# Single-bank accumulators for the last stage, and an order of all steps that comes from a table

## The chip, the cores and the metric

The kernel runs on one core of a Trainium2 chip. Its engines work side by side, each through its own instructions in order: TensorE (PE in the profile; its loading of weights is PEld), VectorE (DVE), ScalarE (ACT), GpSimd (POOL) and SyncE (SP). GpSimd and SyncE issue most of the transfers. The matrix results land in PSUM, of which the kernel's program uses eight banks of 512 float32 columns over 128 partitions. The metric is the device time of one execution in microseconds; a lower one is better.

## What is computed

```python
# q, k, v: [8, 12, 448, 64], scaled by 0.1;  w_ch1: [768, 3072], w_ch2: [3072, 768]
scores = scale * np.matmul(q, k.transpose(0, 1, 3, 2))
attn = np.maximum(scores, 0.0) ** 2 / S
x = np.matmul(attn, v)                      # then [8, 448, 768]
X = np.fft.fft(x, axis=1)
X = np.fft.fft(X, axis=2)
u = x + np.real(X)
un = (u - mean(u)) / np.sqrt(var(u) + 1e-06)
out = u + np.maximum(un @ w_ch1, 0.0) @ w_ch2
```

Eight sequences (batches) go through an attention with a squared relu, a Fourier mixing over the sequence and the channels of which only the real part is kept, a normalisation, and a feed-forward part of two large products with a residual.

## The kernel before, in words

**Stages.** Per batch, heads are taken in pairs. q and k are loaded in row order and turned for TensorE (L623 does it by matmuls with an identity, L593 by transposing transfers); L954 forms the scores of a block of 128 keys, L967 puts a relu on them (ScalarE), L984 or L981 squares them (VectorE or ScalarE), L827 multiplies by v. L822 and L689 to L796 form sums and differences of channels (the Fourier transform is done on halves and quarters), L1432 and L1029 are the products with the cosine matrices, L1252 to L1277 put the parts together into the rows u, L1284 to L1290 find their mean and variance, L1287 (L1065 in batch 0) is the square root on ScalarE, and L1303 (L1102, L1107) writes the normalised rows `un`. These are turned: L1130, L1135 and L1205 by TensorE, L1380 by a transposing transfer from DRAM; the result is `unT`. L400 is a small activation that brings ScalarE the table of the square root.

**Feed-forward part.** The rows of all batches are cut into groups of 256 to 384 columns. A group's first product is L1930, whose results L1915 (VectorE) or L1917 (ScalarE) take out of PSUM with a relu into hidden rows `hT`; L1958, L1985 and L2071 are the second products, in chains of 12 to 24 matmuls, which the adds of L1623 (VectorE) sum onto the residual rows `o`. The two last pairs of groups (four groups in all) are computed as two joints: `joint()` at L1733 forms seven products where eight would be plain, from sums and differences of rows and weights. Each product of L1762 is three matmuls of 256 columns. Between products that go on in the same PSUM bank ScalarE copies the bank's state to SBUF (L1777), and VectorE adds a copy and a bank to the hidden rows (L1782); L1806 is the last relu of a bank.

**PSUM.** `BS` (L237) hands out three tiles of two banks each, `psS`; `BF` two tiles of one bank, `psF`. In the last stage `spread()` (L1708) takes the three two-bank tiles for good and hands out their six halves one by one, with the two `BF` tiles as seventh and eighth bank. The halves are views of one tile, and the order between a writer and a reader is kept by tile: a write to one half waits for the readers of the other half too.

**What sets the order.** Everything is written as generators. Each step says which engine it takes, for how long, what it depends on and which buffers it needs: `need(engine, dur, deps, bufs, ok)`. `Streams.run()` (L102) holds a modelled clock for each engine and always picks the step that could begin first, ties by rank; `HEAD` moves the start of some kinds of steps in some phases, and TensorE takes a filler step where the next would come more than 0.5 us later. What is picked is issued at once, so this sets each engine's order of instructions. Generators also choose by this clock: which of two engines does an eviction, a square or an add (`sooner`, L973), which bank or buffer is taken (`take`, L49), whether a chain opens in the wide tiles.

## Time and profile before

| | |
|---|---|
| median of three runs | 568.57 us (567.13 to 569.33) |
| span of the profiled execution | 566.4 us |
| TensorE busy, share | 556.5 us, 98% |
| VectorE busy, share | 436.2 us, 77% |
| ScalarE busy, share | 318.2 us, 56% |
| GpSimd busy, share | 195.9 us, 35% |
| moved from and to DRAM over the span | 82.41 MB, 157 GB/s |

The profiled execution's own time is its span of 566.4 us, which is 2.2 us under the median. A matmul's duration in the trace reaches until its results are in PSUM, so that consecutive ones overlap. In a row of the trace stand start, length, engine, line, what is written and read, how many instructions, and in brackets how long the engine had been idle before and on what. An idle time on the engine that is not the bound costs nothing by itself.

### The profile page before, as it was taken

The numbers are of one execution on the slowest core, as the hardware profiler recorded it, in microseconds if no ns is written. First come the engines' busy times: TensorE is split into PE (matmuls) and PEld (weight loads), VectorE is DVE, ScalarE is ACT, GpSimd is POOL, SyncE is SP. The second block draws the span as 40 slices with busy tenths as digits, with TensorE's granted clock in tenths as the row PEclk, the third lists the DMA queues.
The fourth block names the chain that finished last, engine by engine and source line by source line (L and its number), as shares of the span: only waits on it lengthen the run. The fifth ranks groups of instructions, "written<-read, shape, count | busy, mean of one in ns | idle before, by whom it ended". The sixth has DMA issues, their size and how long they took to land.

```text
span 566.4 us, 11147 instructions
## 1 busy us (share of the span) xinstructions
PE 556.5 (98%) x4171; PEld 350.1 (62%) x4171; DVE 436.2 (77%) x1016; ACT 318.2 (56%) x536; POOL 195.9 (35%) x281
## 2 busy tenths in 40 slices
PE   7999999999999999999999999999999999999997
PEld 4376556544465455556756757767678688668864
DVE  7976564987789978887997896888899957644762
ACT  5978762676745686585786637638515154015400
POOL 8966225523346234462545545222015000000000
PEclk9999999999999999999999999999999999999999
DMA  9999999979959988899899979956425421231012
GB/s 110 180 209 230 215 215 165 217 144 134 181 96 210 215 117 179 164 187 184 174 163 196 198 121 198 164 123 154 115 65 174 124 75 29 71 127 56 1 57 83
DMA packets 152688, 82.41 MB, mean 146 GB/s; under 512 B 118076, under 2 KB 147900, under 8 KB 152636
## 3 DMA queue, kind: packets, MB, share of 16 engines
q0 software_dynamic: 57056, 33.63, 43.0%
q1 hardware_dynamic: 95580, 48.09, 38.1%
q8 instruction: 32, 0.52, 0.4%
q14 instruction: 20, 0.16, 0.1%
HBM read 62.91 MB, written 26.25 MB: 157 GB/s over the span
## 4 chain that ended last, share of the span: by engine, by line
PE 86%; DMA 5%; DVE 4%; ACT 2%; POOL 1%; issue 1%; DVEq 0%; POOLq 0%; ACTq 0%
PE psF L1930 25%; PE psF L2071 20%; PE psS L1762 8%; PE psS L954 7%; PE psS L2071 5%; DMA kn<-in_k_dram 5%; PE psF L827 5%; PE psF L1985 4%; PE psS L1432 2%; PE psF L1762 2%; PE psF L1958 2%; PE psF L822 1%; PE psF L623 1%; DVE sq L984 1%; PE psS L827 1%
## 5 line engine op out<-in xcount | busy, mean ns | idle before, releaser
L1930 PE MATMUL psF<-unT,w 128*128 128x256 bf16 (+2 forms) x1152 | 165.3, 299 | 0.0
L967 ACT ACTIVATE sq<-psS 128x896 bf16<-128x896 f32 x168 | 144.1, 919 | 31.7 <-PE psS L954 31.2
L1930 PEld LDWEIGHTS <-w 128*128 128x128 bf16 x1152 | 110.9, 98 | 49.6 <-issue 5.2
L984 DVE TENSOR_TENSOR sq<-sq 128x896 bf16<-128x896 bf16 x144 | 88.9, 634 | 13.3 <-ACT sq L967 12.5
L2071 PEld LDWEIGHTS <-hT 128*128 128x128 bf16 x648 | 62.5, 98 | 44.1 <-issue 4.8
L1917 ACT ACTIVATE hT<-psF 128x512 bf16<-128x512 f32 (+2 forms) x121 | 59.6, 508 | 41.1 <-PE psF L1930 40.3
L1623 DVE TENSOR_TENSOR o<-psF,o 128x384 f32<-128x384 f32 (+1 forms) x78 | 42.6, 547 | 24.3 <-PE psF L2071 20.8
L2071 PE MATMUL psF<-w,hT 128*128 128x384 bf16 x336 | 59.7, 326 | 0.6 <-DVE o L1623 0.6
L954 PE MATMUL psS<-qkT 64*128 64x448 bf16 (+1 forms) x336 | 51.5, 354 | 1.0 <-DVE qkT L630 0.8
L1777 ACT COPY copies<-psS 128x256 f32<-128x256 f32 x57 | 19.9, 374 | 53.0 <-PE psS L1762 48.1
L689 DVE TENSOR_SCALAR xT<-psF 128x224 bf16<-128x224 f32 x60 | 20.6, 384 | 26.1 <-PE psF L827 26.1
L1275 POOL TENSOR_TENSOR u<-tp,xn 112x385 f32<-112x385 f32 (+2 forms) x14 | 14.5, 1037 | 72.6 <-DVE tp L1255 48.6
L476 POOL DMA_DIRECT2D qn<-in_q_dram x21 | 15.7, 747 | 57.7 <-DVE qkr L583 50.3
L827 PE MATMUL psF<-sq,vn 128*64 128x448 bf16 x246 | 33.0, 362 | 0.0
L954 PEld LDWEIGHTS <-qkT 64*128 64x128 bf16 (+1 forms) x336 | 12.9, 94 | 32.3 <-issue 26.4
L1762 PEld LDWEIGHTS <-w 128*128 128x128 bf16 x288 | 28.2, 98 | 4.7 <-issue 1.1
L451 POOL DMA_DIRECT2D kn<-in_k_dram x42 | 25.9, 626 | 10.3 <-DMA w<-in_moe_w_ch_dram 6.0
L1284 DVE BATCH_NORM_STATS2 stats<-u 112x6 f32<-112x384 f32 (+2 forms) x56 | 28.7, 543 | 0.8 <-POOL u L1275 0.6
L451 POOL DMA_DIRECT2D vn<-in_v_dram x42 | 26.1, 638 | 6.2 <-DMA w<-in_moe_w_ch_dram 5.4
L476 POOL DMA_DIRECT2D vn<-in_v_dram x24 | 18.9, 789 | 25.5 <-PE psS L954 25.4
L1303 ACT ACTIVATE un<-u,small 112x768 bf16<-112x768 f32 (+2 forms) x22 | 22.0, 1023 | 9.5 <-DVE small L1290 8.4
L1782 DVE CUSTOM_DVE_ANT_0 hT<-psS,copies 128x256 bf16<-128x256 f32 x37 | 15.0, 421 | 14.1 <-PE psS L1762 6.2
(238 smaller groups left out, 946.9 us busy)
## 6 DMA issues: line engine op xcount, KB each, us to landing
out_dram<-o SPq DMA_DIRECT2D x55, 192.0 KB, 2.3
qn<-in_q_dram POOLq DMA_DIRECT2D x21, 224.0 KB, 5.1
vn<-in_v_dram POOLq DMA_DIRECT2D x24, 192.0 KB, 5.6
w<-in_moe_w_ch_dram POOLq DMA_DIRECT2D x12, 384.0 KB, 11.8
w<-in_moe_w_ch_dram POOLq DMA_DIRECT2D x4, 1152.0 KB, 23.4
kn<-in_k_dram POOLq DMA_DIRECT2D x21, 192.0 KB, 5.9
utop<-u SPq DMA_DIRECT2D x12, 336.0 KB, 2.9
o<-utop SPq DMA_DIRECT2D x16, 192.0 KB, 3.7
```

Source lines behind the costliest of these rows:

```text
L451: nc.gpsimd.dma_start(out=t[par * Dh:(par + 1) * Dh, par::2], in_=at)
L476: nc.gpsimd.dma_start(out=to, in_=src[b, hs, 0:rows].rearrange("h (p j) d -> p h (j d)", j=j))
L827: nc.tensor.matmul(av[h * Dh:(h + 1) * Dh, 0:S], lhsT=vn_home[:, at:at + Dh], rhs=sq[:, h, :], start=start, stop=stop, skip_group_check=True)
L954: nc.tensor.matmul(sc[:, h, 0:S].rearrange("k (c q) -> k c q", c=4), lhsT=flat[ps, k0:k0 + KB], rhs=qT[ps, pair], start=True, stop=True)
L967: nc.scalar.activation(r, sc[:, :, 0:S], AF.Relu)
L984: nc.vector.tensor_tensor(r, r, r, op=ALU.mult)
L1284: nc.vector.bn_stats(stats[:n, hf, :], u[:n, hf * (D // 2):(hf + 1) * (D // 2)])
L1623: nc.vector.tensor_tensor(o[:, cols], pc[:, cols], o[:, cols], op=ALU.add)
L1762: nc.tensor.matmul(ps[:, 0:N], lhsT=lhs, rhs=rhs[:, m], start=(start and m == 0), stop=(stop and m == 2), skip_group_check=True)
L1917: nc.scalar.activation(hs, ps, AF.Relu)
L1930: nc.tensor.matmul(ph[:, i * N:(i + 1) * N], lhsT=w1_sb[m][hf][:, (jj + i) * 128:(jj + i + 1) * 128], rhs=unT[:, m, 0:N], start=(m == 0), ...
L2071: nc.tensor.matmul(pc[:, cols], lhsT=lhs[i], rhs=rhs[i][:, cols], start=(start and i == 0), stop=(i == KP - 1), skip_group_check=True)
```

## The change

Two things are changed. First, in the last stage: the wide tiles are taken from a pool of their own, which `spread()` closes once they are free; a new pool gives six tiles of one bank each. The six banks are the same; what differs is that each is a tile by itself.

```diff
+    wide = tc.psum_pool(name="pw", bufs=1)
+    wide_psum = wide.__enter__()
...
-    BS = Banks(3, lambda i: psum.tile([128, 2, 512], FP32, name="psS", tag=f"S{i}", bufs=1))
+    BS = Banks(3, lambda i: wide_psum.tile([128, 2, 512], FP32, name="psS", tag=f"S{i}", bufs=1))
...
         yield need("PE", 0.0, rows_mixed, [BS] * 3)
-        tiles, plain = [BS.take() for _ in range(3)], []
-        B8 = Banks(6, lambda i: tiles[i // 2][:, i % 2] if i < 6 else plain[i - 6])
+        plain = []
+        wide.__exit__(None, None, None)
+        ones = ctx.enter_context(tc.psum_pool(name="p1", bufs=1))
+        B8 = Banks(6, lambda i: ones.tile([128, 512], FP32, name="psS", tag=f"one{i}", bufs=1) if i < 6 else plain[i - 6])
```

Second, `run()` doesn't choose any more. A string of codes names, step by step, the place in the list of the generator that goes next; a second table overrides choices of engine, bank or buffer by a running count of the questions asked. Both were found beforehand by a local search.

```diff
-HEAD = {('attentions', 'PE', 2): -0.6, ('attentions', 'PE', 3): -0.6, ('attentions', 'PE', 4): 0.07, ('mix_rows', 'PE', 2): -0.05}
-PHASES = (48.0, 140.0, 290.0, 440.0)
+CODES = '0123456789ABCDEFGHIJKLMNOPQRSTUVWXY'
+ORDER = "".join((
+    '00900000020099999999999999999999991999999199991999991N102999999190992011OON011111MMF11F4400M4MMF',
...
+CHOICES = {
+    77: 2, 91: 0, 93: True, 98: 1, 107: 0, 121: False, 166: False, 177: False, 190: True,
...
+def chosen(x):
+    asked[0] += 1
+    return CHOICES.get(asked[0] - 1, x)
...
     def run(self):
         end = {}
-        while self.streams:
+        for code in ORDER:
...
-            if best[1][2][0] == "PE" and spare is not None and best[0][1] - spare[0][1] > 0.5:
-                best = spare
-            s = best[1]
+            s = self.streams[CODES.index(code)]
...
-        return wait[other] + d + SPARE < wait[usual] + du
+        return chosen(wait[other] + d + SPARE < wait[usual] + du)
```

Counted over the program, each engine has as many instructions of each line as before (one filler matmul of L2154 is added at the start). What is moved is the order: on TensorE 1790 rows out of 8344 stand in other places, on VectorE 569 of 1018, on ScalarE 205 of 538, on GpSimd 24 and on SyncE 239. From about 100 us on TensorE's order is the old one but for local exchanges, apart from the last stage. Lines in the new file are 48 to 52 higher: L2123 is L2071, L1814 is L1762, L1002 is L954, L1829 is L1777.

Near 258 us of the trace a product of the second feed-forward product follows on TensorE on one that ends in the bank that an add (L1623) has to empty. Before (`w_3`, `w_0`: quarters of a weight matrix; `hT`: hidden rows; the bracket is the engine whose semaphore it waits for):

```order
L2071 MATMUL psF<-w_3_1061,hT 128x384
L2071 LDWEIGHTS hT
L2071 MATMUL psF<-w_3_1061,hT 128x384
L2071 LDWEIGHTS hT
L2071 MATMUL psF<-w_3_1061,hT 128x384
L2071 LDWEIGHTS hT
L2071 MATMUL psF<-w_0_976,hT 128x384 [waits DVE_49]
```

The same place on TensorE in the new order, from behind the first of the score matmuls that follow the last `w_3` matmul:

```order
L1002 LDWEIGHTS qkT
L1002 MATMUL psS<-qkT 128x448
L1002 LDWEIGHTS qkT
L1002 MATMUL psS<-qkT 128x448 [waits Activation_49]
L1002 LDWEIGHTS qkT
L1002 MATMUL psS<-qkT 128x448
L1002 LDWEIGHTS qkT
L1002 MATMUL psS<-qkT 128x448 [waits Activation_49]
L1002 LDWEIGHTS qkT
L1002 MATMUL psS<-qkT 128x448
L2123 LDWEIGHTS hT
L2123 MATMUL psF<-w_0_1008,hT 128x384 [waits DVE_49]
```

Six score matmuls have moved in between the product and the one that waits for its add.

In the second batch's normalisation, near 98 to 103 us, ScalarE had this order before (`qs`: part of the mixed rows; `small`: mean and deviation of a block of rows):

```order
L1252 ACTIVATE qs<-psS 128x385
L1252 ACTIVATE qs<-psS 112x385
L1287 ACTIVATE small<-small,few 128x1 x2
L1303 ACTIVATE un<-u,small 128x768 x2
L1287 ACTIVATE small<-small,few 112x1
L1210 CAST unT<-psS 128x6x127
```

And ScalarE has this now:

```order
L1302 ACTIVATE qs<-psS 128x385
L1337 ACTIVATE small<-small,few 128x1
L1302 ACTIVATE qs<-psS 112x385
L1353 ACTIVATE un<-u,small 128x768
L1337 ACTIVATE small<-small,few 128x1
L1353 ACTIVATE un<-u,small 128x768
L1337 ACTIVATE small<-small,few 112x1
```

Each block's root now stands directly ahead of that block, but for one eviction, where two roots stood ahead of two blocks.

In the last stage, near 514 us, TensorE before (`chan`, `sumx`: buffers that hold normalised rows or their differences here; `w_n`: weights):

```order
L1762 MATMUL psF<-chan_116,w_0_0_477 128x256
L1762 LDWEIGHTS w_1_0_487
L1762 MATMUL psF<-chan_116,w_1_0_487 128x256
L1762 LDWEIGHTS w_2_0_495
L1762 MATMUL psF<-chan_116,w_2_0_495 128x256
L1762 LDWEIGHTS w_3_0_505
L1762 MATMUL psS<-sumx,w_3_0_505 128x256 [waits DVE_49]
```

The same product (the one with `sumx`) on TensorE now:

```order
L1814 MATMUL psS<-chan_119,w_0_0_439 128x256 [waits DVE_49]
L1814 LDWEIGHTS w_1_0_456
L1814 MATMUL psS<-chan_119,w_1_0_456 128x256
L1814 LDWEIGHTS w_2_0_493
L1814 MATMUL psS<-chan_119,w_2_0_493 128x256
L1814 LDWEIGHTS w_3_0_506
L1814 MATMUL psS<-sumx,w_3_0_506 128x256 [waits DVE_49]
```

It stands behind another product, and its wait is for the reader of its own bank, no longer for the reader of a second half.

73 lines of the change are left out of this document (46 added, 27 removed), and 18 rows, old and new, of the table CHOICES.

## Prediction, made before the changed kernel ran

> **What bounds the kernel now.** I read the page's busy shares first, then what TensorE waited for, then the stretches of the span around the longest of those waits.
>
> ```profile
> span 566.4 us, 11147 instructions
> ...
> PE 556.5 (98%) x4171; PEld 350.1 (62%) x4171; DVE 436.2 (77%) x1016; ACT 318.2 (56%) x536; POOL 195.9 (35%) x281
> ...
> PE 86%; DMA 5%; DVE 4%; ACT 2%; POOL 1%; issue 1%; DVEq 0%; POOLq 0%; ACTq 0%
> ```
>
> TensorE is busy 98% of the span, and the chain that ended last lies 86% on it. The last step is the sum's anchor: 566.4 us of span against a median of 568.57, so 2.2 us lie around the span or are this execution's luck, and I carry them along unchanged. TensorE is idle 566.4 - 556.5 = 9.9 us. A change that neither removes nor adds a matmul that matters can win from waits, not from work.
>
> ```profile
> 0.00:10.40 10.40, 7.62 (x69) 4.72 (x69) 7.58 (x21) 4.66 (x7) 9.12 (x19) 1.00 0.86 92
> ...
> 29.80:47.62 17.82, 17.26 (x202) 13.08 (x201) 12.83 (x37) 13.55 (x29) 10.90 (x15) 1.00 1.09 224
> 47.62:430.00 382.38, 380.31 (x2728) 225.94 (x2726) 311.45 (x709) 240.68 (x368) 150.54 (x191) 1.00 0.98 166
> 430.00:566.40 136.40, 132.01 (x1010) 98.15 (x1008) 86.00 (x213) 40.02 (x108) 6.76 (x6) 1.00 0.25 77
> ```
>
> In this table of stretches (window, its length, then the busy time of TensorE and of the other engines; the granted clock, third from the end, is full throughout) 2.8 us of the idle time lie before 10.4 us, 0.6 us between 29.8 and the first product of the feed-forward part at 47.62, 2.1 us in the next 382 us, and 4.4 us in the last stage and the tail. The list of waits names them:
>
> ```profile
> PE psS L1205 <- ACT un L1303: 1.0, 1, 1.0
> PE psF L2071 <- DVE o L1623: 0.9, 2, 0.6
> ...
> PE psS L1762 <- DVE hT L1782: 0.5, 2, 0.3
> ```
>
> A matmul is shown longer than it keeps the next from starting: of L2071 below, five stand in 0.98 us, each 0.326 long, so they start 0.163 apart. I therefore price a wait by the distance of two starts less the usual distance, which makes it 0.16 (L2071) or 0.15 to 0.17 (L1762) longer than the idle time printed.
>
> **The change, part by part.** The engines keep the same instructions, apart from one more filler matmul (L2154) at the start, where the tensor engine has nothing to do before the first data; it costs nothing. Engine choices come out with equal counts on each engine. So all terms are waits that go or come.
>
> *1. Single-bank tiles in the last stage (L1708 to L1715).* Before, two products share one tile, and the write of one waits for the reader of the other's half. Four places in the last stage show it:
>
> ```profile
> 475.61 0.49 PE L1762 MATMUL psS<-unT,w 128*128 128x256 bf16 x3
> ...
> 476.09 0.27 PE L1762 MATMUL psS<-unT,quarter 128*128 128x256 bf16 x1
> ...
> 514.04 0.49 PE L1762 MATMUL psF<-chan,w 128*128 128x256 bf16 x3
> ...
> 514.36 0.41 DVE L1782 CUSTOM_DVE_ANT_0 hT<-psS,copies 128x256 bf16<-128x256 f32 x1
> ...
> 514.83 0.60 PE L1762 MATMUL psS<-sumx,w 128*128 128x256 bf16 x4 [0.30 <-DVE hT L1782]
> ...
> 522.47 0.37 ACT L1777 COPY copies<-psS 128x256 f32<-128x256 f32 x1 [0.51 <-DVE hB L1782]
> 522.47 0.38 PE L1762 MATMUL psS<-chan,xT 128*128 128x256 bf16 x2
> ...
> 522.89 0.49 PE L1762 MATMUL psS<-sumx,w 128*128 128x256 bf16 x3
> ...
> 535.45 0.38 PE L1762 MATMUL psS<-chan,xT 128*128 128x256 bf16 x2
> ...
> 536.02 0.49 PE L1762 MATMUL psS<-chan,w 128*128 128x256 bf16 x3 [0.19 <-DVE hT L1782]
> ```
>
> Three matmuls that start 0.11 apart (0.49 = 2 x 0.11 + 0.27) would let the next start 0.33 after the first: expected 475.94, 514.37, 522.69 and 535.67, seen 476.09, 514.83, 522.89 and 536.02. The waits are 0.15 + 0.46 + 0.20 + 0.35 = 1.16 us, and in all four the reader waited for reads the other half. They go: -1.15.
>
> The new order of that stage is tighter, though. A product that continues in the same bank needs the copy of L1777 (or the relu of L1806) first. Before, 3 products of L1762 stand only two products (0.65 us) behind the end of the one whose copy they need; in the new order I count 16. The nearest case in the trace:
>
> ```profile
> 477.07 0.49 PE L1762 MATMUL psS<-sumx,w 128*128 128x256 bf16 x3
> ...
> 477.60 0.38 ACT L1806 ACTIVATE hB<-psS 128x256 bf16<-128x256 f32 x1
> ...
> 478.05 0.49 PE L1762 MATMUL psS<-chan,w 128*128 128x256 bf16 x3
> ```
>
> The product issued from 477.07 leaves the queue at 477.40, ScalarE reads it 477.60 to 477.98, and the next use starts at 478.05, 0.65 us later and without an extra wait. So such a spot costs nothing if ScalarE is free and what ScalarE still has to do if not. At 4 of the 16 the row ahead on ScalarE belongs to a product that ended only one product, 0.33 us, earlier; a copy of 0.37 then ends 0.04 late, and a start 0.05 late adds to it. From below the price is 0 (this row), from above a whole copy each, 16 x 0.37 = 5.9 us (the row at 522.47). It is nearest to the first, ScalarE being busy 40 of 136 us in this stretch: 4 x 0.09 + 12 x 0.01, about +0.5.
>
> *2. Order at 258 us.* A product of group chain L2071 takes the bank that VectorE's add L1623 must empty first, straight behind the product that the add reads:
>
> ```profile
> 257.22 0.98 PE L2071 MATMUL psF<-w,hT 128*128 128x384 bf16 x5
> ...
> 258.24 0.56 DVE L1623 TENSOR_TENSOR o<-psF,o 128x384 f32<-128x384 f32 x1
> ...
> 258.85 0.65 PE L2071 MATMUL psF<-w,hT 128*128 128x384 bf16 x3 [0.65 <-DVE o L1623]
> ```
>
> Start to start this costs 0.81 us. In the new order six score matmuls (L954) stand between: at 0.19 us a matmul (two of them in 0.38 us, from 49.24 to 49.62 below), some of them side by side, about 0.8 us in all. The next is late only if the add waits for a VectorE row ahead of it: -0.75, between -0.81 and 0.
>
> *3. Second normalisation of batch 1 at 102 us.* The turn L1205 waits for the row block L1303 on ScalarE:
>
> ```profile
> 93.75 0.43 DVE L583 COPY qkr<-kn 128x1024 bf16<-128x1024 bf16 x1 [1.48 <-DMA kn<-in_k_dram]
> 94.09 0.55 DVE L1255 TENSOR_TENSOR tp<-psS,qs 128x385 f32<-128x385 f32 x1
> ...
> 98.97 0.29 ACT L1287 ACTIVATE small<-small,few 128x1 f32<-128x1 f32 x1 [6.11 <-DVE small L1285]
> 101.11 0.29 ACT L1287 ACTIVATE small<-small,few 128x1 f32<-128x1 f32 x1 [1.85 <-DVE small L1285]
> 101.96 1.94 ACT L1303 ACTIVATE un<-u,small 128x768 bf16<-128x768 f32 x2 [0.55 <-DVE small L1290]
> ...
> 103.04 0.51 PE L1205 MATMUL psS<-ident,un 128*128 128x128 bf16 x6 [0.97 <-ACT un L1303]
> ```
>
> VectorE stands 1.48 us before the copy that waits for a load, and everything for the block is queued behind it; ScalarE takes both roots before the first block. In the new order L1255 and L1257 stand ahead of that copy, the same two for the other rows behind the first root, and the first block straight behind that root. From root to block took 101.96 - 101.40 = 0.56 us, so the block could start at 98.97 + 0.29 + 0.56 = 99.8, less 1.48 and two VectorE rows of 0.55: 97.2, and ends 0.97 later, at 98.2. The turn stands 18 matmuls of 0.163, 2.9 us, earlier: TensorE would come to it at 103.04 - 1.13 - 2.9 = 99.0, with 0.8 us to spare. The second block hangs on GpSimd's rows, ahead of which two load issues fewer stand, and comes out just about when TensorE needs it. Best case -1.13; worst, if loads land no earlier and the turn moves up 2.9 us, about +0.8 (2.9 less the 2.1 that the roots alone give). I take -0.6.
>
> *4. The head.* The root table (L400) moves behind the first copy of L1081:
>
> ```profile
> 35.37 1.28 ACT L400 ACT_TABLE_LOAD   x1
> ...
> 37.37 0.32 PE L1029 MATMUL psS<-pc,seqm 128*128 128x384 bf16 x1 [0.24 <-ACT u L1081]
> ```
>
> That wait (0.40 start to start) goes, and the last products of the channel stage stand a little earlier; but what TensorE turns next is set by GpSimd's three blocks, in order behind load issues:
>
> ```profile
> 42.27 0.98 POOL L1102 TENSOR_SCALAR un<-u,small 112x768 bf16<-112x768 f32 x1
> ```
>
> It ends at 43.25. Between 0 and -0.9 of the head can go (the 0.40 here, and 0.5, the largest other thing in this stretch, its 0.56 us of idle time); I take -0.4, this wait alone. Against it stand 16 transposes (L623) moved from behind the first half product (L1930) to ahead of it:
>
> ```profile
> 48.69 0.39 PE L623 MATMUL psF<-ident,qn 112*64 112x112 bf16 x8
> ...
> 48.80 0.56 DVE L1915 TENSOR_SCALAR hT<-psF 128x384 bf16<-128x384 f32 x1
> ...
> 49.24 0.55 PE L954 MATMUL psS<-qkT 128*128 128x448 bf16 x2
> 49.62 0.81 PE L1930 MATMUL psF<-unT,w 128*128 128x384 bf16 x4
> ```
>
> As work this is neutral. As cover it isn't: they hide L1915, which empties the bank that the next L1930 takes. Now only the two L954 (49.24 to 49.62, 0.38 us) do; TensorE would stand there at 48.69 + 0.38 = 49.07, VectorE is through at 49.36 and some 0.06 of signalling: +0.35, between 0 and +0.6.
>
> *5. The moved loads and transposes.* GpSimd's issues keep their order in the head; SyncE's are moved in 56 places, each of which keeps more distance than its transfer needs, but one: a transpose L1380 (unT) has about 5 us of matmuls between issue and first use where it had 11.
>
> ```profile
> DMA to landing us min/median/max: 2.3/3.4/6.9
> ```
>
> At the median it is in time, at the longest it costs 6.9 - 5.0 = 1.9. I take 0. All other swaps stand at 0; nothing in the trace prices them, so I bound them by the waits not named so far, 2.1 - 1.6 = 0.5 gained, and by one more wait like L1205's, 1.0 lost.
>
> Sum: -1.15 + 0.5 - 0.75 - 0.6 - 0.4 + 0.35 = -2.05. 568.57 - 2.05 = 566.5.
>
> **The rivals.** *Slower: the tight copies queue.* If ScalarE starts each of the 16 copies behind another one, each costs up to 0.37: 568.57 - 2.55 (the sum without its 0.5) + 5.9 = 571.9. For it speaks that relus and copies share ScalarE and arrive in twos; against it the spare time of that engine. It eats the whole gain from 0.16 us a spot, and makes the kernel slower by over 0.5% from (2.55 + 2.84) / 16 = 0.34.
>
> *No change: waits only move.* The loads set when batch 1's blocks and the head's blocks are ready (the 1.48 us before L583). If parts 3 and 4 give nothing, the L1915 wait comes and a transpose is late by its 1.9 us, the sum is -1.15 + 0.5 - 0.75 + 0.35 + 1.9 = +0.85, 569.4; without the late transpose 567.5.
>
> *Faster: each term at its good end.* -1.16 - 0.81 - 1.13 - 0.9 - 0.5 = -4.5, with no new wait: 564.1. For it: ScalarE's spare time, and the 9.9 us idle. Against: it needs all five.
>
> *TensorE isn't the bound at all.* The page "Perfetto Trace Analysis" of the Trainium skill (section "Identifying the Most-Contended Engine") says that matmul busy time is no measure of nearness to the limit and that the share of weight loading is better; by that, 62% (the row above), an order could win up to 566.4 - 350.1 = 216 us. The rows speak against it here: the five matmuls of 257.22 start 0.163 apart, evenly, so the columns stream without a gap. A time under 560 by this gets 0.01.
>
> **How the numbers follow.** Chances: forecast 0.46 (its own range 565.2 to 568.0), waits that move 0.18, faster 0.23, slower 0.12, the last one 0.01. The measurement can't tell less than about 0.5%, 2.84 us, from no change: the runs shown already spread over 567.13 to 569.33. Faster by more (under 565.73) is the faster rival and 0.05 of the forecast's own range, with the last one 0.29; slower by more is the slower rival and 0.02 of late transposes, 0.14; the rest 0.57. The range of 8 in 10 goes from 563.6, just under the faster rival, to 570.4, halfway to the slower one.
>
> **What the profile after would show.** Right: no wait of L1762 on a sum or copy of another product; no idle time before L2071 near 257 us; L1205 with under 0.3 us; a wait of some 0.2 us printed for L1930 on L1915 near 49 us. The chain of waits in the last stage would name ScalarE's copies L1777 with 0.1 us or less at a time. Wrong: L1762 idle for L1777 with more than 0.1 us at many places, or new waits on loads between 100 and 300 us, or a first product of the feed-forward part well after 47.6.

## The result: 0.7% slower, and the profile after

The changed kernel takes 572.15 us (median of four runs, 571.42 to 573.25) against 568.03 us for the kernel before in the same series: a ratio of 1.0072 with a 95% interval of 1.0051 to 1.0093, 4.1 us slower. The forecast was 566.5. The profiled execution took 572.8 us with a span of 571.0.

```profile
span 571.0 us, 11108 instructions
...
PE 555.1 (97%) x4167; PEld 351.5 (62%) x4172; DVE 431.8 (76%) x1016; ACT 317.8 (56%) x536; POOL 200.7 (35%) x281
...
PE 75%; DVE 6%; POOL 6%; issue 4%; DMA 4%; SPq 2%; ACT 1%; DVEq 0%; POOLq 0%; ACTq 0%
```

These are the span, the busy shares and the chain that ended last. TensorE has the same work; the chain lies 75% on it instead of 86%, and VectorE, GpSimd, transfers and issue have the rest. To see where, I cut both spans at the same three matmuls. The table of stretches of the kernel after (window, length, then busy time and number of instructions, TensorE first; granted clock third from the end):

```profile
0.00:49.45 49.45, 43.70 (x455) 27.24 (x455) 37.91 (x96) 38.31 (x61) 41.11 (x84) 1.00 1.11 171
49.45:285.26 235.81, 233.23 (x1578) 127.93 (x1581) 185.07 (x433) 153.56 (x237) 98.48 (x131) 1.00 1.09 172
285.26:451.68 166.42, 162.79 (x1254) 110.09 (x1253) 140.41 (x310) 93.66 (x144) 61.07 (x66) 1.00 0.81 152
451.68:571.00 119.32, 115.42 (x888) 86.22 (x885) 68.38 (x179) 32.23 (x96) 0.00 (x0) 1.00 0.22 67
```

The stretch of the kernel before that answers to the third line:

```profile
284.00:446.00 162.00, 161.79 (x1254) 109.91 (x1252) 140.00 (x310) 92.94 (x143) 58.91 (x65) 1.00 0.79 151
```

The four lengths were 47.62, 236.38, 162.00 and 120.40 before. So the head (all that comes before the first L1930) is 1.83 us longer, the next stretch 0.57 shorter, the third 4.42 longer and the last 1.08 shorter, 4.60 in sum, which is the difference of the spans. Part of the first two is work that changed sides: the 16 transposes L623 that the prediction named now stand in the head. In the third, TensorE had 0.21 us of idle time before and has 3.63 now. The list of waits names what ended them:

```profile
PE psF L1982 <- DMA unT<-nbot: 1.2, 1, 1.2
PE psF L2123 <- ACT hT L1969: 1.2, 1, 1.2
PE psF L1982 <- DVE hT L1967: 1.0, 2, 0.8
PE psS L1457 <- DVE fold L796: 1.0, 1, 1.0
PE psS L875 <- DVE sq L1034: 0.9, 1, 0.9
...
PE psS L1079 <- DVE small L1123: 0.7, 1, 0.7
```

L1982 is L1930 of the kernel before, L2123 is L2071, L1969 is L1917 and L1967 is L1915, L1457 is L1407, L796 is L748, L875 is L827, L1034 is L984, L1079 is L1029 and L1123 is L1073. None of these waits stood in the list of before, and none is a product of the last stage. The table prices the larger waits by the distance of two starts less the usual one, as in the prediction:

| place in the kernel after | what TensorE waits for | us |
|---|---|---|
| 32, 35 and 39 us, head | VectorE's folds, ScalarE's copies, the mean of a row block | 1.17, 0.82, 0.87 (the last was 0.40) |
| 51 and 55 us | relu L1915, relu L1917 on ScalarE | 0.43 and 0.94 |
| 200 us | a transposed group (`unT`) | 1.30 |
| 290 and 295 us | VectorE's copy L689, add L1623 | 0.44 and 0.37 |
| 341 us | VectorE's square L984 | 1.06 |
| 394 us | relu L1915 on VectorE | 0.93 |
| 444 and 447 us | relu L1917 on ScalarE, add L1623 | 1.37 and 0.40 |

The rows from 290 us on add up to 4.57 us, where the profile of before had one wait of some 0.3 us (at 296 us). That is nearly the whole of the 4.42 us of the third stretch.

Two rows in the head show how a wait arises that no list names as one. GpSimd has a row of two columns there (L411; in the kernel before it is L363):

```profile
25.80 3.48 POOL L411 TENSOR_SCALAR drow<-drow 128x2 f32<-128x2 f32 x1
...
25.12 1.68 DVE L1034 TENSOR_TENSOR sq<-sq 128x896 bf16<-128x896 bf16 x3
...
28.91 0.27 DVE L796 TENSOR_TENSOR fold<-xT 128x225 bf16<-128x225 bf16 x1
31.19 0.41 DVE L421 TENSOR_SCALAR dfty<-dfty 128x480 int32<-128x480 f32 x1 [2.00 <-POOL dfty L414]
```

Before, it took 0.61 us:

```profile
23.95 3.48 DVE L984 TENSOR_TENSOR sq<-sq 128x896 bf16<-128x896 bf16 x6
...
24.57 0.61 POOL L363 TENSOR_SCALAR drow<-drow 128x2 f32<-128x2 f32 x1
```

It now starts beside a run of VectorE rows that stand without a gap from 25.12 to 28.91 + 0.27 = 29.18, and ends at 29.28. VectorE, which needs what GpSimd makes of it, then stands 2.00 us, and the folds behind that row are late for TensorE. The page "SBUF — State Buffer" of the Trainium skill (section "Who interferes with whom") says that a VectorE instruction with two inputs in SBUF and a GpSimd instruction that reads SBUF exclude each other, the second being blocked until the first is through. The row after agrees, and shows more: it is held not for one VectorE row but until a run of twelve pauses. Such a run doesn't always do that, though: before, the same row took 0.61 us in the middle of six squares without a gap. What decides between the two isn't shown.

The other row is the table load that the prediction had going out of TensorE's way:

```profile
37.52 1.28 ACT L1115 ACT_TABLE_LOAD   x1
...
39.53 0.49 PE L1079 MATMUL psS<-pc,seqm 128*112 128x384 bf16 x2 [0.71 <-DVE small L1123]
...
45.33 0.29 ACT L448 ACTIVATE drow<-few 128x1 f32<-128x1 f32 x1
```

The activation that was to bring the table (L400, here L448) only comes at 45.33 us, behind the roots, so that the first root (L1065, here L1115) loads it. The load stands between the first copy and that root, instead of ahead of the copy, and TensorE waits for what comes after the root.

### The profile page after: what moved, and what is told of

It reads as the page before. It is cut to its first block, busy times and chain, and to the rows that moved or that the text cites. A ratio compares the mean times of both kernels' runs of the same rounds, so it can differ in the third digit from the quotient of the medians.

```text
span 571.0 us, 11108 instructions
## 1 busy us (share of the span) xinstructions
PE 555.1 (97%) x4167; PEld 351.5 (62%) x4172; DVE 431.8 (76%) x1016; ACT 317.8 (56%) x536; POOL 200.7 (35%) x281
## 4 chain that ended last, share of the span: by engine, by line
PE 75%; DVE 6%; POOL 6%; issue 4%; DMA 4%; SPq 2%; ACT 1%; DVEq 0%; POOLq 0%; ACTq 0%
PE psF L1982 22%; PE psF L2123 15%; PE psS L1814 8%; PE psS L1002 5%; PE psS L2123 5%; PE psF L2037 4%; PE psF L2010 4%; PE psF L875 4%; PE psF L1814 2%; PE psS L1482 2%; SPq L641 1%; DMA unT<-ntop 1%; PE psF L870 1%; DMA unT<-nbot 1%; POOL qk L524 1%
## 5 line engine op out<-in xcount | busy, mean ns | idle before, releaser
L1982 PE MATMUL psF<-unT,w 128*128 128x256 bf16 (+2 forms) x1147 | 164.8, 299 | 2.5 <-DMA unT<-nbot 1.2
L1982 PEld LDWEIGHTS <-w 128*128 128x128 bf16 x1152 | 110.9, 98 | 52.1 <-issue 8.1
L1034 DVE TENSOR_TENSOR sq<-sq 128x896 bf16<-128x896 bf16 x144 | 87.2, 626 | 12.9 <-ACT sq L1017 12.8
L2123 PEld LDWEIGHTS <-hT 128*128 128x128 bf16 x648 | 62.3, 98 | 45.5 <-issue 4.0
L1969 ACT ACTIVATE hT<-psF 128x512 bf16<-128x512 f32 (+2 forms) x121 | 59.6, 509 | 39.2 <-PE psF L1982 38.2
L2123 PE MATMUL psF<-w,hT 128*128 128x384 bf16 x336 | 60.2, 326 | 1.5 <-ACT hT L1969 1.2
L1002 PE MATMUL psS<-qkT 64*128 64x448 bf16 (+1 forms) x336 | 51.4, 354 | 1.3 <-ACT sq L1017 0.8
L1829 ACT COPY copies<-psS 128x256 f32<-128x256 f32 x57 | 20.0, 375 | 48.5 <-PE psS L1814 47.9
L524 POOL DMA_DIRECT2D kn<-in_k_dram x21 | 16.0, 764 | 49.3 <-DVE qkr L631 41.1
L1002 PEld LDWEIGHTS <-qkT 64*128 64x128 bf16 (+1 forms) x336 | 13.0, 94 | 32.7 <-issue 28.2
L875 PE MATMUL psF<-sq,vn 128*64 128x448 bf16 x246 | 32.7, 362 | 0.0
L1814 PEld LDWEIGHTS <-w 128*128 128x128 bf16 x288 | 28.2, 98 | 3.8
L499 POOL DMA_DIRECT2D kn<-in_k_dram x42 | 25.8, 621 | 9.2 <-PE psS L1002 5.3
L499 POOL DMA_DIRECT2D vn<-in_v_dram x42 | 26.5, 640 | 5.0 <-DMA w<-in_moe_w_ch_dram 3.8
L875 PEld LDWEIGHTS <-vn 128*64 128x64 bf16 x288 | 13.0, 108 | 21.5 <-issue 17.5
```

Of the source, the lines that this page charges most:

```text
L499: nc.gpsimd.dma_start(out=t[par * Dh:(par + 1) * Dh, par::2], in_=at)
L524: nc.gpsimd.dma_start(out=to, in_=src[b, hs, 0:rows].rearrange("h (p j) d -> p h (j d)", j=j))
L875: nc.tensor.matmul(av[h * Dh:(h + 1) * Dh, 0:S], lhsT=vn_home[:, at:at + Dh], rhs=sq[:, h, :], start=start, stop=stop, skip_group_check=True)
L1002: nc.tensor.matmul(sc[:, h, 0:S].rearrange("k (c q) -> k c q", c=4), lhsT=flat[ps, k0:k0 + KB], rhs=qT[ps, pair], start=True, stop=True)
L1034: nc.vector.tensor_tensor(r, r, r, op=ALU.mult)
L1814: nc.tensor.matmul(ps[:, 0:N], lhsT=lhs, rhs=rhs[:, m], start=(start and m == 0), stop=(stop and m == 2), skip_group_check=True)
```

## The experiments

All runs write the order as a list of step names, so that stretches of the old and of the new order can be joined and single steps moved. In these kernels lines are 747 to 753 higher than in the kernel before. In most of them L2824 is L2071, L2683 is L1930, L2670 is L1917, L2668 is L1915, L2531 is L1782, L2374 is L1623, L2054 and L2051 are L1303 and L1300, L2038 is L1287, L2035 is L1284, L2026 and L2028 are L1275 and L1277, L2006 and L2008 are L1255 and L1257, L2003 is L1252, L1991 is L1240, L1735 is L984, L1718 is L967, L2183 is L1432, L1529 is L780, L2800 and L2802 are L2047 and L2049, L2040 and L2041 are L1289 and L1290, L2131 and L1342 are the transposes L1380 and L593, L2092 is L1341, a transfer that GpSimd issues, and L1200 is L451, the issue of a load. Times are compared by their ratios to the kernel before, which was run beside each.

### The two parts apart, and the last stage

The old order with single-bank tiles:

```diff
-ORDER = <steps of the new table>
+ORDER = <steps in the order of the kernel before>
```

> The old order on every engine, step for step, and only the six single-bank tiles of the last stage. If the waits on the other half are what the first term said, this gives -1.15 us against the kernel before (567.4 to 566.9, ratio about 0.998), and the four waits near 476, 515, 523 and 536 us are gone. If the new tiles cost something by themselves (the rival: the change itself, not the order, is what slows the kernel), it is 568 or more.

Measured 567.02 us, ratio 0.9985 (0.9959 to 1.001). In its trace the last stage is 1.17 us shorter than before, and L1762 waits for no sum of another product.

The new order with the old tiles of two banks:

```diff
-        ones = ctx.enter_context(tc.psum_pool(name="p1", bufs=1))
-        B8 = Banks(6, lambda i: ones.tile([128, 512], FP32, ...) if i < 6 else plain[i - 6])
+        tiles, plain = [BS.take() for _ in range(3)], []
+        B8 = Banks(6, lambda i: tiles[i // 2][:, i % 2] if i < 6 else plain[i - 6])
```

> The new order on every engine with the old two-bank tiles. If the order carries the whole loss and the tiles a small gain, this is the changed kernel's 572.15 plus the waits on other halves, which this order, being tighter, has more of: 573.3 to 575. If the tiles are the loss, it is near 568.

590.46 us, ratio 1.039 (1.0364 to 1.0417): 18 us more than the kernel after, and far above what was expected. What the halves cost depends on the order: 1.15 us in the old one, 18 in the tighter one. The list of waits has what the single banks remove (L2511 and L2531 are L1762 and L1782):

```profile
PE psS L2511 <- DVE hT L2531: 5.8, 7, 2.2
```

The old order up to the last stage, the new order in it:

```diff
-ORDER = <steps of the new table>
+ORDER = <old order, 2387 steps> + <new order of what is left>
```

> The old order up to the last stage, then the new order of the last stage with single-bank tiles. If a copy 0.65 us ahead of its reader costs nothing on a free ScalarE, this equals the kernel with the old order and single-bank tiles within 0.5 us (566.9 to 567.4). If the 16 tight places queue (the rival that forecast slower), they cost 0.1 to 0.37 us each: 568.5 to 572.

566.96 us, ratio 0.9981 (0.9971 to 0.9991), its last stage 1.12 us shorter than before. So by the traces the tiles give what was forecast, 1.15 us (in the times, the interval of the old order with single banks still holds no change); the new order of that stage gives nothing on top with single banks, and its tighter copies cost nothing.

### The head

The old order for the first 60 us, then the new one:

```diff
-ORDER = <steps of the new table>
+ORDER = <old order, 418 steps> + <new order of what is left>
```

> The old order up to about 60 us (batch 0 and the first products of the feed-forward part), the new order for all that is left. If the head's waits are a loss by themselves, the 2.6 us that the changed kernel is behind at 60 to 80 us go and stay gone: about 569.5. If later stages had slack that hides a late head, or the loss simply comes back (the rival), it stays at 571.5 to 572.5.

571.82 us, ratio 1.0062 (1.0043 to 1.008). The first L1930 still comes 1.07 us later than in the profile of before: the same order varies by that much. What the new order loses in the head is got back later: in the run below with the new order up to 284 us, whose head comes 1.80 us late, the matmuls of 130 us stand where they stood before, since L1205 doesn't wait at 102 us. That wait hangs on loads, as the prediction showed, and isn't a fixed one: in nine runs whose order was the old one there it was between 0 and 1.12 us, 0.67 in the middle (1.13 in the profile of before).

The kernel after without GpSimd's row of two columns (its factor goes into the next row as a second operation):

```diff
-        nc.gpsimd.tensor_scalar(drow[:, 0:2], drow[:, 0:2], 1.0 / S, None, op0=ALU.mult)
...
-            nc.gpsimd.tensor_scalar(..., drow[:, i:i + 1], None, op0=ALU.mult)
+            nc.gpsimd.tensor_scalar(..., drow[:, i:i + 1], 1.0 / S, op0=ALU.mult, op1=ALU.mult)
```

> The kernel after without the GpSimd row L363 of two columns in the head (its factor 1/S goes into the next row, L366, as a second operation of the same instruction). If that row is held up as such, and VectorE waits for GpSimd for it, the first L1930 comes about 1 us earlier and the time is near 571.1, provided nothing absorbs it. If any GpSimd row at that place is held up while VectorE streams, L366 takes the time instead and the time stays within 0.4 us of 572.15.

571.33 us, ratio 1.0075 (1.005 to 1.01). VectorE no longer waits for GpSimd (L1121 is L373):

```profile
29.85 0.39 DVE L1121 TENSOR_SCALAR dfty<-dfty 128x480 int32<-128x480 f32 x1
```

The first L1930 comes 0.64 us earlier than in the kernel after, but the ratio is no better. The row's delay is real; that it costs time at the end isn't shown.

### Mending the waits where they are printed

ScalarE's relu that TensorE waits for at 444 us, ahead of the roots:

```diff
-L2670 ACTIVATE hT<-psF 128x512 x4
+L2670 ACTIVATE hT<-psF 128x512 x5
 L2038 ACTIVATE small<-small,few 112x1 x2
-L2670 ACTIVATE hT<-psF 128x512
```

> The kernel after with one relu (the ScalarE half of L1917 that the wait at 443.4 us names) issued ahead of the root L1287 it stood behind. If the wait there is a loss of its own, TensorE gets 1.2 to 1.4 us back and the time is about 570.9. If something else, a transfer or a late row, stands right behind it, the wait turns up under another name within the next 20 us and the time stays at 571.9 to 572.3.

572.18 us, ratio 1.0085 (1.0061 to 1.011): nothing is won. In its trace TensorE runs on for 24 matmuls, and then waits as long for another row:

```profile
441.65 4.06 PE L2824 MATMUL psF<-w,hT 128*128 128x384 bf16 x24
446.94 1.14 PE L2824 MATMUL psF<-wsum,s 128*128 128x384 bf16 x6 [1.23 <-DVE o L2374]
```

Four places at once:

```diff
 <the relu as above>
 L2028 TENSOR_TENSOR u<-tp,xn 112x383
+L2668 TENSOR_SCALAR hT<-psF 128x512
 L2035 BN_STATS stats<-u 112x6 x2
 L2036 BN_AGGR small<-stats 112x2
-L2668 TENSOR_SCALAR hT<-psF 128x512
...
-L2026 TENSOR_TENSOR u<-tp,xn 112x385
 L2092 DMA nbot_102<-un,backs 384x768
 L1200 DMA kn<-in_k_dram 64x2x64 x2
+L2026 TENSOR_TENSOR u<-tp,xn 112x385
...
-L1342 DMA_TRANSPOSE qkT<-qkr 128x8x112
-L1342 DMA_TRANSPOSE qkT<-qkr 128x8x128
 L2131 DMA_TRANSPOSE unT<-ntop_91 128x6x224
 L2131 DMA_TRANSPOSE unT<-nbot_99 128x6x160
+L1342 DMA_TRANSPOSE qkT<-qkr 128x8x112
+L1342 DMA_TRANSPOSE qkT<-qkr 128x8x128
```

> Four places of the kernel after mended at once: the relu at 443.4 us, the relu at 393.8 us ahead of two L1284 rows, the two qkT transposes at 188 us behind the two unT ones, and the GpSimd row L1275 at 340 us behind two load issues. Each alone measured in the trace: 1.37, 0.93, 1.2 and 1.24 us. If the loss of the new order is the sum of such places, 572.15 - 4.7 = 567.4 (566.9 to 568.2). If the places share one limit behind them (loads or ScalarE), at most half comes back: 569.8 or more.

571.12 us, ratio 1.0062 (1.0043 to 1.0081), far from 567.4. At 341 us the cause is plain. In the kernel after:

```profile
340.11 1.59 DVE L1034 TENSOR_TENSOR sq<-sq 128x896 bf16<-128x896 bf16 x1
...
340.28 0.92 POOL L1325 TENSOR_TENSOR u<-tp,xn 112x385 f32<-112x385 f32 x1
```

With GpSimd's row behind the two load issues:

```profile
338.37 0.61 DVE L1735 TENSOR_TENSOR sq<-sq 128x896 bf16<-128x896 bf16 x1
```

1.59 us beside GpSimd's row, 0.61 without it; and the long one ends at 341.70, 0.50 us after GpSimd's row (341.20), about its own length. That wait shrank from 1.06 to 0.08 us, but the moved GpSimd row stretches later VectorE rows, and 0.52 us comes up at 345. The stretching itself isn't new: in the profile of before, VectorE's L1275 takes 1.83 us from 336.80 on beside a row of GpSimd. In the new order it falls on a square that TensorE needs at once. At 394 us the mended relu hands the wait to one of ScalarE's, behind a row L1303 (L2054 there) that waits for VectorE:

```profile
393.56 1.03 ACT L2054 ACTIVATE un<-u,small 112x768 bf16<-112x768 f32 x1 [0.97 <-DVE small L2041]
394.49 0.57 ACT L2670 ACTIVATE hT<-psF 128x512 bf16<-128x512 f32 x1
...
395.12 2.12 PE L2683 MATMUL psF<-unT,w 128*128 128x256 bf16 x18 [0.76 <-ACT hT L2670]
```

The transposes at 200 us: the same wait is 1.30, 0.75 and 0.43 us in three runs with the new order there, and absent in four others, so that what the move gave can't be told from the transfers' own variation. At 314 us another group (`qkT`) keeps TensorE idle for 0.94, 1.37 and 1.30 us in the runs with two-bank tiles, with the old head and with the relu alone, and in none of six others with the new order there, the kernel after among them.

### Parts of the new order in the old one

The old order with single banks, the steps of 83 to 137 us in the new order, and the score product at 258 us moved by hand:

```diff
-ORDER = <steps of the new table>
+ORDER = <old> + <steps 523 to 790 in the new order> + <old, chain step 1411 ahead of score step 1404>
```

> The order of before with only three things of the change: single-bank tiles in the last stage, the steps of about 83 to 137 us in the new order, and the score product at 258 us behind the first product of its group chain. If the three terms of the prediction that the trace bore out are the change's whole gain and independent of the rest: 567.0 (old order, single banks) - 0.8 (258 us) - 0.4 to -1.1 (102 and 124 us) = 565.4 to 565.8. If the gain at 102 us is taken up by the wait for loads as in the old order, 566.2; 567 if both are.

569.77 us, ratio 1.0042 (1.0019 to 1.0066). The 1.00 us won by 130 us stays up to 258 us, where 3.5 us are lost:

```profile
257.56 0.62 DVE L1735 TENSOR_TENSOR sq<-sq 128x896 bf16<-128x896 bf16 x1 [2.16 <-ACT sq L1718]
...
259.08 0.55 DVE L2374 TENSOR_TENSOR o<-psF,o 128x384 f32<-128x384 f32 x1
```

The scores come later, so ScalarE's relus L967 on them come later, and VectorE, which has the squares of them ahead of the add, waits 2.16 us in order. TensorE waits 2.49 us for the add. I had moved one step and left its readers where they were. The same with the add ahead of the squares:

```diff
+L2374 TENSOR_TENSOR o<-psF,o 128x384
 L1735 TENSOR_TENSOR sq<-sq 128x896
 L1519 TENSOR_TENSOR fold<-folds 128x684
 L1735 TENSOR_TENSOR sq<-sq 128x896
-L2374 TENSOR_TENSOR o<-psF,o 128x384
```

> The run before it with one thing mended: VectorE's add of the chain (L1623 at 258 us) stands ahead of the squares L984 of the scores that were moved, as in the new order, where in the run before it stood behind them and waited 2.2 us for ScalarE's. If that row alone made the loss of 3.5 us there, the gains stay (-1.0 at 102 to 124 us, -0.8 at 258, -1.1 in the last stage): about 2.7 to 2.9 us under the time of before, near 565. If gains of the middle are swallowed by a wait that the old order has later, 566 to 567.

567.17 us, ratio 0.9984 (0.9971 to 0.9998): the loss is gone, but not 565. The wait at 258 us is gone too; the next one, for VectorE's folds, which the same squares now push back, is 1.76 us, more than the 0.65 that the move was to save. And L1205 waits 0.64 and 1.87 us at 100 and 105 us in spite of the new order. There VectorE stands 2.23 us for a load at 93 us; the profiled execution is the slowest of eleven (570.36 us), so how much of this the median has isn't shown:

```profile
263.98 0.46 PE L2183 MATMUL psS<-chan,fold 128*114 128x193 bf16 x3 [1.76 <-DVE fold L1529]
```

The new order up to 284 us, then the old one; and the other way round, only 284 to 450 us new:

```diff
+ORDER = <new, 1551 steps> + <old order of what is left>
...
+ORDER = <old, 1550 steps> + <steps 1550 to 2362 in the new order> + <old>
```

> The new order for all steps up to about 284 us, from there the old order, single-bank tiles. If the loss is made by rows that stand wrongly between 284 and 450 us, this one is not slower than before: 567.0 (old order, single banks) less 0.5, give or take the 0.8 by which the head varies, 565.7 to 567.5. If the new order carries a backlog out of its first half (loads issued later, a late head), the old second half shows it as waits of its own and the time is 569 or more.

> The old order with single-bank tiles and only the steps of about 284 to 450 us in the new order. If the loss is made there: 567.0 + 0.57 + 1.24 + 0.93 + 1.37 + 0.40 = 571.5, with the four places at 290, 340, 393 and 443 us showing the waits they show in the kernel after. If it is a backlog from the first half, at most two of them show and the time is under 569.

567.76 us, ratio 0.9995 (0.9983 to 1.0006), and 571.28 us, ratio 1.0066 (1.0042 to 1.009). The second has the four largest waits of the kernel after between 284 and 450 us, of the same size: 1.06, 0.93, 1.36 and 0.40 us. The expected one at 290 us it hasn't; instead 0.45 us come up at 326. Against the old order with single banks (567.02) it costs 4.3 us, without the new order ahead of it, so that stretch makes the loss by itself.

The first run is 0.7 us above 567.02, with intervals that overlap. Its trace says that this isn't lost in the first half: the first L2071 behind 284 us starts at 283.23 us, where it started at 284.34 before, and 1.0 us of that lead is gone by 297, most of it in a wait where the orders are joined that is larger than in the kernel after (0.90 against 0.44 us):

```profile
288.09 1.15 PE L2824 MATMUL psF<-w,hT 128*128 128x384 bf16 x6 [0.74 <-DVE xT L1438]
```

(L1438 is L689.) In all six runs with the whole new order up to 284 us that matmul stands 0.3 to 1.3 us earlier than in the profile of before. In the profile of the kernel after it stands 1.26 us later; that execution has waits of 0.94 us at 55 and of 1.30 at 200 us that none of the six has in this size. Eight of nine runs with the old order up to there stand between 1.1 us earlier and 0.1 later, the ninth, after a late load, 1.8 later. That 0.7 and 4.3 add up to about the kernel after's loss is therefore partly luck.

### The largest wait, 1.77 us at 443 and 447 us

Only the steps of 440 to 450 us new, and then those of 419 to 450 us:

```diff
+ORDER = <old, 2306 steps> + <steps 2306 to 2362 in the new order> + <old>
...
+ORDER = <old, 2226 steps> + <steps 2226 to 2362 in the new order> + <old>
```

> The old order with single-bank tiles and only the steps of about 440 to 450 us in the new order: VectorE's two adds L1623 behind two rows L1661, and a relu L1917 behind two roots L1287. No matmul is moved. If these rows make the waits at 443 and 447 us by themselves: 567.0 + 1.4 to 1.8, about 568.6. If the waits come from what the new order did before, nothing: 567.0.

> The old order with single-bank tiles and only the steps of about 419 to 450 us in the new order. The stretch 440 to 450 alone made no wait; 284 to 450 made 1.77 us at 443 and 447. If the cause is the last normalisation, whose GpSimd row L1300 stands 2.9 us later against TensorE because a root L1287 was put behind two relus at 434 us, the whole 1.77 us is here: 566.7 + 1.8 = 568.5. If it is what the order before 419 us leaves behind (ScalarE and VectorE full from 380 to 400 us), nothing: 566.7.

566.7 us, ratio 0.9972 (0.9957 to 0.9988), without any wait there; and 568.18 us, ratio 1.0008 (0.9999 to 1.0018), with the whole 1.77 us. So the rows at which the wait is printed are not its cause. It comes from a batch's last normalisation, ahead of which something was moved. The rows of the second run, from the first link to the last:

```profile
421.66 1.47 PE L2683 MATMUL psF<-unT,w 128*128 128x256 bf16 x12
422.97 0.49 PE L1991 MATMUL psS<-pc,seqh 114*113 114x385 bf16 x2
...
424.02 0.56 DVE L2006 TENSOR_TENSOR tp<-psS,qs 113x385 f32<-113x385 f32 x1 [1.59 <-ACT qs L2003]
...
433.18 1.99 POOL L2051 TENSOR_SCALAR un<-u,small 113x768 bf16<-113x768 f32 x1 [4.13 <-DVE small L2041]
435.25 1.09 POOL L2026 TENSOR_TENSOR u<-tp,xn 112x385 f32<-112x385 f32 x1
...
436.38 1.02 DVE L2035 BATCH_NORM_STATS2 stats<-u 112x6 f32<-112x384 f32 x2 [0.81 <-POOL u L2026]
...
441.19 0.99 PE L2824 MATMUL psF<-w,hT 128*128 128x384 bf16 x5 [1.20 <-ACT hT L2670]
```

VectorE stands 1.59 us for the first sequence product (L1240), which the new order puts behind 12 matmuls L1930; a root L1287 stands behind two relus, so that GpSimd's L1300 is late; VectorE stands 0.81 us for GpSimd; the roots that follow are late, and with them the relu in ScalarE's order that TensorE needs. First the second root alone, with the two small rows of VectorE that need it:

```diff
-L2038 ACTIVATE small<-small,few 113x1
-L2670 ACTIVATE hT<-psF 128x512 x2
-L2038 ACTIVATE small<-small,few 113x1
+L2038 ACTIVATE small<-small,few 113x1 x2
+L2670 ACTIVATE hT<-psF 128x512 x2
```

> The run before it with one root L1287 ahead of the two relus L1917 it was put behind (434 to 436 us), and VectorE's two small rows that need it up by the same distance. If that root is the cause: GpSimd's L1300 starts 2 us earlier, VectorE's wait of 0.81 us for GpSimd's L1275 goes, and 0.8 to 1.8 us come back: 566.7 to 567.7. If VectorE's own work is too much there, the wait at 443 stays: 568.5.

568.42 us, ratio 1.0001 (0.9983 to 1.0019). GpSimd's rows come 2 us earlier and VectorE doesn't wait for them, but now VectorE's rows meet GpSimd's:

```profile
435.09 0.85 POOL L2028 TENSOR_TENSOR u<-qs,xn 112x383 f32<-112x383 f32 x1
...
434.64 1.73 DVE L2026 TENSOR_TENSOR u<-qs,xn 112x385 f32<-112x385 f32 x1
```

1.73 us for a row that took 0.56 in the run before it, ending 0.43 us after GpSimd's. Of 1.77 us of waiting 1.46 are left. The same root, and GpSimd's row at 340 us, in the run with 284 to 450 us new:

```diff
 <the root as above>
-L2026 TENSOR_TENSOR u<-tp,xn 112x385
 L2092 DMA nbot_102<-un,backs 384x768
 L1200 DMA kn<-in_k_dram 64x2x64 x2
+L2026 TENSOR_TENSOR u<-tp,xn 112x385
```

> The run with the steps of 284 to 450 us in the new order (571.28), with the root of 434 us mended as in the run before this and GpSimd's row L1275 at 340 us behind the two load issues. Alone they cost 1.77 and 1.24 us in that run. If both causes are right: 571.28 - 3.0 = 568.3; if the waits come back under other names within the next microseconds, as they did when the relu at 443 and the relu at 393 us were moved: 570.5 or more.

569.9 us, ratio 1.0033 (1.002 to 1.0046): about half of what was expected. In its trace the wait at 341 us is gone and 0.52 us come up at 345; at 443 us 1.47 are left of 1.77. Next the sequence products alone, in the run with 419 to 450 us new:

```diff
-L2683 MATMUL psF<-unT,w_0_0_480 128x256
...
 L1991 MATMUL psS<-pc,seqh 114x385
+L2683 MATMUL psF<-unT,w_0_0_480 128x256
...
```

> The run with only the steps of 419 to 450 us in the new order (568.2), with the two sequence products of batch 3 (L1240) put back ahead of the 12 matmuls L1930 they had been moved behind, and ScalarE's copy L1252 of the second ahead of one relu. In that run VectorE waits 1.59 us for the copy of the first product and has no other pause up to the wait at 443 us. If these 12 matmuls are the cause, the 1.77 us at 443 and 447 us go: 566.4 to 566.9. If VectorE's rows are too many in any case, at least half of the wait stays: 567.5 or more.

567.92 us, ratio 1.0004 (0.9995 to 1.0013). The pause of 1.59 us is down to 0.28, but VectorE then stands 0.70 us for the first root and again 0.81 for GpSimd:

```profile
429.30 0.16 DVE L2040 RECIPROCAL small<-small 113x1 f32<-113x1 f32 x1 [0.70 <-ACT small L2038]
```

1.64 us are left. The same moves, with the product at 386 us and GpSimd's row at 340 us, in the kernel after itself:

```diff
 <L1991 at 386, 427 and 432 us ahead of 12 matmuls L2683 each>
 <L2003 ahead of one relu L2670, twice>
 <L2026 at 340 us behind two issues, as above>
```

> The kernel after with the same moves, the same for the product L1240 at 386 us (and its copy L1252 ahead of one relu), and GpSimd's row L1275 at 340 us behind two load issues. If sequence products put behind matmuls L1930 make the waits at 394 and 443 us: 572.15 - 0.93 - 1.77 - 0.5 to 1.24 (340 us) = 568.2 to 569.0. If moved rows only hand the waits on, as in the earlier mends: 570.5 or more.

571.45 us, ratio 1.0066 (1.0051 to 1.0081), a miss. The wait at 394 us went from 0.93 to 0.28 us, so there the late product is a cause; the one at 443 us stays at 1.25 and 0.40, as in the run before. Last, both links at once, in the run with 419 to 450 us new. The second root goes ahead of three relus here, and the first one ahead of one:

```diff
 L2670 ACTIVATE hT<-psF 128x512 x3
 L2003 ACTIVATE qs<-psS 112x385
-L2670 ACTIVATE hT<-psF 128x512 x2
-L2038 ACTIVATE small<-small,few 113x1
-L2670 ACTIVATE hT<-psF 128x512 x2
-L2038 ACTIVATE small<-small,few 113x1
+L2670 ACTIVATE hT<-psF 128x512
+L2038 ACTIVATE small<-small,few 113x1 x2
+L2670 ACTIVATE hT<-psF 128x512 x3
```

> The run before it that had the sequence products back (419 to 450 us in the new order otherwise), and both roots L1287 of the block ahead of the relus they stood behind, with VectorE's two small rows that need the second. Alone, the products gave 0.1 to 0.2 us of the wait and the root 0.3. If the wait at 443 us is the end of a chain in which every link had been put behind something, and all its links are now mended, it goes: 566.6 to 567.0. If VectorE's rows, stretched beside GpSimd's, fill the time they win, at least 1 us of it stays: 567.7 or more.

566.54 us, ratio 0.997 (0.9956 to 0.9985). TensorE runs through and waits 0.16 us, 0.32 from start to start, instead of 1.77:

```profile
439.75 4.06 PE L2824 MATMUL psF<-w,hT 128*128 128x384 bf16 x24
443.97 1.14 PE L2824 MATMUL psF<-wsum,s 128*128 128x384 bf16 x6 [0.16 <-DVE o L2374]
```

The products alone gave 0.1 us and the second root alone 0.3; all together gave 1.45. What the first root has in it isn't shown. (The profiled execution, 569.17 us, is the slowest of twelve: TensorE stands 1.50 us for a load at 91 us.) This is also one of four runs that beat both kernels with an interval that leaves out no change; the others are the old order with the new last stage (0.9981), that with 440 to 450 us new (0.9972) and that with the parts at 83 to 137 and 258 us (0.9984). Their intervals overlap: what they share, single banks and the old order nearly throughout, is worth 0.2 to 0.3%.

## Why the prediction was wrong, point by point

- **The sum.** The forecast was 2.05 us less, the kernel takes 4.1 more. The tiles gave their -1.15. The order up to 284 us was forecast at -1.4 (parts 2, 3 and 4) and gave nothing that is clear of noise in the times. The order from 284 to 450 us was forecast at nothing and costs 4.3.
- **TensorE bounds the kernel, and the change moves waits only.** Nothing speaks against it. Its busy time is 555.1 us against 556.5. That it could be far from its limit had 1 chance in 100; no run took less than 565.7 us.
- **Part 1, single-bank tiles, -1.15 with +0.5 for tight copies.** The first was right (1.17 and 1.12 us in two runs). The second was sized wrongly: it is 0. The rival that let these copies queue for 571.9 us came near the time by another cause.
- **Part 2, 258 us, -0.75.** Right at its place: TensorE loses 0.81 us less there. The run that did the move by hand shows why it went well in the new order only: VectorE's add stands ahead of the squares there.
- **Part 3, 102 us, -0.6.** Right in kind, L1205 doesn't wait, and 1.13 us by the two profiles. But the wait of before was itself between 0 and 1.13 us from run to run, so that on average less was to be won, and in the first run with the new steps of 83 to 137 us it still waits 0.59.
- **Part 4, the head, -0.4 and +0.35.** The second was right (0.43). The first failed in sign: the table load doesn't leave the path, since L400 moves behind all the roots and not only behind one copy. The load moves from ahead of a copy to ahead of a root, and 0.40 us become 0.87. That GpSimd's row would be held up was not seen at all. In the time the head cost little, since L1205's wait takes a late head in.
- **Part 5, "All other swaps stand at 0", with 1.0 lost at the worst.** This is the step that failed. The swaps of 284 to 450 us cost 4.3 us: at six places TensorE waits for a row of VectorE or ScalarE that comes late. Shown to the end is the largest, 1.77 us: a product and two roots put behind other rows. The part had bounded them by one more wait like L1205's, though the idle time of that stretch in the profile of before, 0.21 us in 162, says that there is nothing to win there and anything to lose. It also named a late transpose with 1.9 us as its bound; at 200 us it is 1.30 us in the profile after and 0 to 0.75 in other runs.
- **The rivals.** "Waits only move" had the right idea for the head and the wrong place for the loss. The slower one had 0.12, as one mechanism in the last stage; a rival was missing in which the rows moved on VectorE, ScalarE and GpSimd cost time in the one stretch that had no slack.
- **What the profile after would show.** The signs of being right came for the last stage, for 257 us, for L1205 at 102 us and for L1915. Of the signs of being wrong two came: a wait for a transfer at 200 us, and a first L1930 at 49.45 instead of 47.6.

What stays open: mending the wait at 341 us brought 0.52 us up at 345, and that at 394 us was made smaller only, so that no run removed their cost wholly. What parts 2 and 3 are worth in the time is open too: the run with both, and the old order elsewhere, takes 567.17 us against 567.02 without them, but its trace has other waits in place of the gains.

## What to carry to other kernels

When a change moves hundreds of rows, cut the span into stretches, and price each by its slack: where the bound engine had no idle time, a new order can only lose. To find the cause of a loss, join the two orders at a step where nearly the same work is done, and halve; then look whether the join itself makes a wait. The row at which a wait is printed is the last link; mending it alone hands the wait on to another row, and a moved step must take its readers on the other engines along.

## What had not been expected of the hardware

- A row can wait without any wait being printed: it is shown as long. GpSimd's row of two columns took 3.48 us instead of 0.61, VectorE's square 1.59 instead of 0.61 and its add L1275 1.73 instead of 0.56, each beside rows of the other engine, and each through within 0.50 us of the end of the other's. By the trace the two VectorE rows begin 0.17 and 0.45 us ahead of the GpSimd row beside them, so the printed starts don't tell which one is held.
- The same order doesn't give the same waits. The head's end moved by 1.07 us and the wait for loads at 102 us by 1.13 us between runs, and a transposed group kept TensorE waiting for 0 to 1.30 us, while the medians of the kernel before lay between 567.4 and 568.6 us in all series.
